# An FFT filter feeding a two-matmul block: where the second half of a complex product is formed

## The chip, the cores and the metric

The kernel runs on one core of one Trainium2 chip. The metric is device time in microseconds (us) of one execution; the median of three runs of the kernel before is 816.59 us (816.1 to 817.59). Engines are named as the profile names them: PE is TensorE (matmuls), PEld its weight loads, DVE is VectorE, ACT is ScalarE, POOL is GpSimd, SP is SyncE. POOL and SP do nothing here but issue DMAs. Each has its own DMA queue.

## The reference, cut to what matters

```python
def _attn_ref(x, filt_r, filt_i):              # x: (8, 3008, 256)
    X = np.fft.rfft(x, axis=1)                 # 1505 frequencies
    Y = X * (filt_r + 1j * filt_i)[None]       # complex product
    return np.fft.irfft(Y, n=3008, axis=1)

def _moe_ref(x, w_in, w_out, alpha):           # x: (24064, 256)
    h = x @ w_in                               # 256 -> 2048
    g = np.maximum(h, 0.0) + alpha * np.minimum(h, 0.0)
    return g @ w_out                           # 2048 -> 256
```

The output of the first, reshaped to 24064 rows, is the input of the second.

## The kernel before, in words

**The FFT of one batch** (`class Fft`; b counts 0 to 7) splits 3008 into 47 x 64 and 1505 frequencies into 24 groups ("k1"). It runs in pieces:

- `piece_a` (16 of them, L156): one matmul of the loaded input `xs` into one of the two PSUM buffers named psF, evicted by ACT into `asb`. After every fourth, `save_a` (L165) stores a quarter of `asb` to DRAM (`a_dram`) through SP's queue, 384 KB.
- `turn_a` (L169): four DMAs of 384 KB on SP's queue read `a_dram` back transposed into `at`, in runs of 512 bytes.
- `piece_b` (12, each two k1, L178): two matmuls give the spectrum in a psF buffer, real parts on partitions 0 to 63 and imaginary parts on 64 to 127. DVE multiplies it twice: `uu` by `filt_s`, `ww` by `filts_s`, 128 x 512 each. For these batches `filt_s` holds the filter's real part on both halves and `filts_s` the imaginary part on both.
- `piece_c` (12, L189): per k1, two accumulating matmuls, `twi_s` with `uu` and `twx_s` with `ww`. `twx_s` is `twi_s` with its halves exchanged and one sign turned, so the second matmul completes the complex product inside the inverse transform. ACT evicts the sum to `v`.
- `turn_c` (4, L202): after each third `piece_c`, four DMAs of 96 KB on SP's queue store that part of `v` to `v_dram`. After the fourth, SP waits until all of these have landed and then loads `zt` in four DMAs of 384 KB (L214).
- `piece_d` (16, L216): four small matmuls from `zt`, evicted by ACT to `yT`. The first four need only the first of the four `zt` loads.

**The two-matmul block** (`class Block`) handles 48 blocks of 512 columns of `yT` (four of 384). `up(j)`, 16 per block, is two matmuls of 512 columns into a buffer hps; after every second one ACT copies the pair to fp16 (`gtb`, a ring of 17 buffers) and DVE does two `TENSOR_SCALAR` (L415) and one add over 1024 elements (L416). `down(q)`, one block later, is four matmuls of 256 columns that read `gtb`; ACT evicts to `osb` (three buffers) twice per block and SP stores it (L388).

**What sets the order.** Everything is written in program order by hand, and each engine works through its own list strictly in that order. The main loop has 768 steps; a step is one `up` and one `down`, followed by whatever `plan` holds for that step. `plan_fft` (L439) enters a batch's pieces: for batches b = 3 to 7, with p = 96 (b - 1), `piece_a` at p - 54 to p - 24 (every second step), `turn_a` at p - 22, `piece_b` at p + 6, p + 11, ... p + 61, each `piece_c` four steps behind its `piece_b`, the last `turn_c` at p + 66, `piece_d` from p + 91. Batch 1 has its `piece_b` every 2.5 steps (44 to 71), batch 2 every 5 (110 to 165). POOL's queue carries the loads of `xs` (`load_x`, L123): two DMAs for each quarter of the next batch, entered one step after the `piece_a` that frees the buffer. So the pieces of batch b + 1 overlap with those of batch b, and SP's queue takes the stores, turns and loads of both in the order in which the steps enter them.

Batch 0 (`class First`) has its own pieces, run before the main loop; it uses `twx_s` too (built by `cross`, L334).

Of the kernel before, what the change touches and what calls it, by code (L numbers as in the profile page):

```python
# [10 lines left out]
FP16 = mybir.dt.float16  # L11
# [5 lines left out]
NK1 = 24  # L17
D = 256
# [4 lines left out]
OP = mybir.AluOpType  # L23
# [41 lines left out]
def kernel(  # L65
# [10 lines left out]
    nc = tc.nc  # L76
# [9 lines left out]
    konst = ctx.enter_context(tc.tile_pool(name="konst", bufs=1))  # L86
    p_x = ctx.enter_context(tc.tile_pool(name="p_x", bufs=4))
    p_fft = ctx.enter_context(tc.tile_pool(name="p_fft", bufs=1))
    p_uw = ctx.enter_context(tc.tile_pool(name="p_uw", bufs=2))
    p_m = ctx.enter_context(tc.tile_pool(name="p_m", bufs=2))  # L90
    p_osb = ctx.enter_context(tc.tile_pool(name="p_osb", bufs=3))
    psH = ctx.enter_context(tc.tile_pool(name="psH", bufs=2, space=bass.MemoryType.PSUM))
# [9 lines left out]
    wi3_s = konst.tile([96, 2 * N1], FP16, name="wi3_s")  # L102
    twf_s = konst.tile([128, NK1, 128], FP16, name="twf_s")
    twi_s = konst.tile([128, NK1, 128], FP16, name="twi_s")
    twx_s = konst.tile([128, NK1, 128], FP16, name="twx_s")
    filt_s = konst.tile([128, NK1, D], FP16, name="filt_s")
    filts_s = konst.tile([128, NK1, D], FP16, name="filts_s")
    al16 = konst.tile([16, 128], FP32, name="al16")
# [5 lines left out]
    wfx_s = konst.tile([2 * N1, 96], FP16, name="wfx_s")  # L114
    id16 = konst.tile([128, 128], FP16, name="id16")
    gtb = konst.tile([128, 17, 2, 512], FP16, name="gtb")
    yT = konst.tile([128, 2, 2 * NFFT], FP16, name="yT")

    def xrow(b, h, c):
# [3 lines left out]
    def load_x(b, c):  # L123
        xs = p_x.tile([2 * N1, 8 * D], FP16, name="xs")
        for h in range(2):
            nc.gpsimd.dma_start(out=xs[h * N1 : h * N1 + N1], in_=xrow(b, h, c))  # L126
        return xs
# [12 lines left out]
    def bank(wide=False):  # L140
        if wide:
            return psH.tile([128, 2, 512], FP32, name="hps")[:, 0]
        return psF.tile([128, 512], FP32, name="psF")


    class Fft:
# [31 lines left out]
        def piece_b(self, kp):  # L178
            px = bank().rearrange("p (k d) -> p k d", k=2)
            for kh in range(2):  # L180
                k1 = 2 * kp + kh
                nc.tensor.matmul(px[:, kh], twf_s[:, k1], self.at[:, k1], start=True, stop=True)  # L182
            uu = p_uw.tile([128, 2, D], FP16, name="uu")
            ww = p_uw.tile([128, 2, D], FP16, name="ww")
            nc.vector.tensor_mul(uu, px, filt_s[:, 2 * kp : 2 * kp + 2])  # L185
            nc.vector.tensor_mul(ww, px, filts_s[:, 2 * kp : 2 * kp + 2])  # L186
            self.uw[kp] = uu, ww

        def piece_c(self, kp, evict, pv=None):  # L189
            if kp == 0:  # L190
                self.v = p_fft.tile([128, NK1, D], FP16, name="v")
                self.zt = p_fft.tile([96, NH, D], FP16, name="zt")
            uu, ww = self.uw.pop(kp)
            if pv is None:
                pv = bank().rearrange("p (k d) -> p k d", k=2)
            for kh in range(2):
                k1 = 2 * kp + kh
                nc.tensor.matmul(pv[:, kh], twi_s[:, k1], uu[:, kh], start=True, stop=False)  # L198
                nc.tensor.matmul(pv[:, kh], twx_s[:, k1], ww[:, kh], start=False, stop=True)  # L199
            evict(self.v[:, 2 * kp : 2 * kp + 2], pv)  # L200

        def turn_c(self, q):  # L202
# [33 lines left out]
    class First(Fft):  # L236
# [27 lines left out]
        def piece_b(self, kp):  # L264
            hp = psH.tile([128, 2, 512], FP32, name="hps")
            px, pz = (hp[:, i].rearrange("p (k d) -> p k d", k=2) for i in range(2))
            for i, ps in enumerate((px, pz)):
                for kh in range(2):
                    k1 = 2 * kp + kh
                    for o in (0, 64):  # L270
                        nc.tensor.matmul(ps[o : o + 64, kh], twf_s[:, k1, 64 * i : 64 * i + 64],
                                         self.at[:, k1], start=True, stop=True)
            uu = p_uw.tile([128, 2, D], FP16, name="uu")
            ww = p_uw.tile([128, 2, D], FP16, name="ww")
            nc.vector.tensor_mul(uu, px, filt_s[:, 2 * kp : 2 * kp + 2])
            nc.vector.tensor_mul(ww, pz, filt_s[:, 2 * kp : 2 * kp + 2])
            self.uw[kp] = uu, ww
# [33 lines left out]
    for g in range(4):  # L311
        ka, kb = 6 * g, 6 * g + 6
# [9 lines left out]
    for q in range(2):  # L322
        nc.gpsimd.dma_start(
            out=wout_s[:, 8 * q : 8 * q + 8],
            in_=moe_w_out[1024 * q : 1024 * q + 1024].rearrange("(j p) d -> p j d", p=128))
# [3 lines left out]
    def warm(n):  # L329
        pw = psO.tile([128, 2, D], FP32, name="op")  # L330
        for _ in range(n):
            nc.tensor.matmul(pw[:, 0, 0:128], id16, id16, start=True, stop=True)

    def cross(ka, kb):  # L334
        nc.vector.tensor_copy(twx_s[0:64, ka:kb], twi_s[64:128, ka:kb])
        nc.vector.tensor_scalar(twx_s[64:128, ka:kb], twi_s[0:64, ka:kb], -1.0, None, OP.mult)
# [16 lines left out]
    for kp in range(12):  # L353
# [4 lines left out]
            f0.piece_b(kp + 2)  # L358
        if kp in (0, 3):
            cross(6 + 2 * kp, 12 + 4 * kp)  # L360
    for o in (0, 64):
        nc.gpsimd.dma_start(out=filts_s[o : o + 64], in_=filt_s[64:128])
    nc.gpsimd.dma_start(out=filt_s[64:128], in_=filt_s[0:64])
    warm(8)
    for i in range(4):
        f0.piece_t(i, both[i % 2], i % 2 == 1)
# [69 lines left out]
    def put(step, fn, *args):  # L436
        plan.setdefault(step, []).append((fn, args))

    def plan_fft(b, a0, ga, ta, b0, gap, d0, quarters=1):  # L439
        f = Fft(b)  # L440
        for i in range(16):
            put(a0 + ga * i, f.piece_a, i, on_act)
        for c in range(4):
            put(a0 + ga * (4 * c + 3), f.save_a, c)
            if b + 1 < NB:
                put(a0 + ga * (4 * c + 3) + 1,
                    lambda b=b, c=c: xc.update({(b + 1, c): load_x(b + 1, c)}))
        for q in range(quarters):
            w = NK1 // quarters
            put(ta, f.turn_a, nc.sync, w * q, w * q + w)  # L450
        for kp in range(12):
            put(int(b0 + gap * kp), f.piece_b, kp)
            put(int(b0 + gap * kp) + 4, f.piece_c, kp, on_act)
        for q in range(4):
            put(int(b0 + gap * (3 * q + 2)) + 5, f.turn_c, q)
        for i in range(16):
            put(d0 + min(i, 4) + 2 * max(i - 4, 0), f.piece_d, i, on_act)

    for g, t0, d0, gap, evs in ((1, 0, 4, 1, both), (2, 17, 24, 2, (on_dve,)), (3, 32, 40, 2, (on_act,))):
        for i in range(4):  # L460
            put(t0 + gap * i, f0.piece_t, 4 * g + i, evs[i % len(evs)])
            put(d0 + gap * i, f0.piece_d, 4 * g + i, evs[i % len(evs)])
    plan_fft(1, 16, 1, 32, 44, 2.5, 92, 4)
    plan_fft(2, 66, 2, 97, 110, 5, 187, 4)
    for b in range(3, NB):
        p = 96 * (b - 1)
        plan_fft(b, p - 54, 2, p - 22, p + 6, 5, p + 91)

    prev = None
    step = 0  # L470
# [43 lines left out]
```

## Time and profile before

| | |
|---|---|
| median of the runs | 816.59 us |
| the profiled execution: its own time, its span | 817.19 us, 815.4 us |
| granted TensorE clock, mean | 0.997 |
| busy: PE, DVE, ACT, POOL | 795.7, 620.2, 594.9, 49.7 us |
| inverse matmuls, L198 and L199 | 168 and 168 of 128 x 256, mean 273 and 272 ns |
| products, L185 and L186 | 84 and 84 of 128 x 512, mean 684 and 681 ns |
| HBM read and written | 55.67 and 46.66 MB |

The page gives one execution. "Busy" is the time in which an engine had at least one instruction under way; matmuls overlap in a pipeline, so the mean duration of one is longer than the distance between two starts. A timeline row gives start, duration, engine, line, what is written from what, how many instructions are merged in it, and in brackets the idle time ahead of it with what ended it. Rows of SPq and POOL are DMA issues, not transfers. A row of the windows view gives for a stretch of the span the busy time of each engine, then the granted clock, the busy share of the 16 DMA engines (above 1 when packets overlap) and GB/s.

### The profile page before, as it was taken

The page shows a single profiled execution, that of the slowest core. Times are in us where ns is not written, and L with a number is a line of the kernel's source. Part 1 is how long each engine was busy: PE and PEld are TensorE (multiplying, and loading weights), DVE is VectorE, ACT ScalarE, POOL GpSimd, SP SyncE. Part 2 cuts the span into 40 slices and gives each one's busy share as a digit, 9 for nine tenths or more (in the row PEclk, how much of TensorE's full clock was granted, in tenths as well). Part 3 has the DMA queues.
Part 4 walks back from the last instruction along what each step waited for, and adds up shares of the span by engine and source line. Part 5 has one row for each costly group of instructions (what it writes and reads, how often), then busy time and mean ns, then how long its engine had stood idle before and what let it go on. Part 6 is the DMA issues. An engine that isn't in the chain of part 4 may idle for free.

```text
span 815.4 us, 16040 instructions
## 1 busy us (share of the span) xinstructions
PE 795.7 (98%) x6117; PEld 557.1 (68%) x6117; DVE 620.2 (76%) x1377; ACT 594.9 (73%) x836; POOL 49.7 (6%) x99
## 2 busy tenths in 40 slices
PE   7889999999999999999999999999999999999997
PEld 6656667676667666776667766767666777776665
DVE  4876886788777887788777887788877788777773
ACT  3677778868777677777877777786777766686663
POOL 7401001000100001000100001000000000000000
PEclk9999999999999999999999999999999999999999
DMA  9977429623692247721584136832255121511111
GB/s 186 195 157 174 123 66 220 168 58 84 139 215 61 69 99 176 174 52 46 134 214 105 46 66 159 199 81 66 74 162 140 47 59 46 136 41 33 40 40 52
DMA packets 88757, 89.76 MB, mean 110 GB/s; under 512 B 8600, under 2 KB 79272, under 8 KB 88488
## 3 DMA queue, kind: packets, MB, share of 16 engines
q1 hardware_dynamic: 79512, 68.80, 31.2%
q0 software_dynamic: 9168, 19.93, 14.6%
q8 instruction: 48, 0.79, 0.4%
q14 instruction: 29, 0.24, 0.1%
HBM read 55.67 MB, written 46.66 MB: 125 GB/s over the span
## 4 chain that ended last, share of the span: by engine, by line
PE 86%; DVE 5%; ACT 3%; DMA 3%; issue 2%; SPq 1%; POOL 0%; ACTq 0%; DVEq 0%; POOLq 0%
PE op L425 37%; PE hps L406 37%; PE psF L162 3%; PE psF L221 2%; PE psF L182 2%; PE psF L199 2%; PE psF L198 2%; DVE gtb L416 1%; DVE m L415 1%; ACT gtb L412 1%; DMA v_dram<-v 1%; DMA xs<-in_x_dram 1%; DMA twf_s<-c_twf 1%; SPq L208 1%; ACT v L228 1%
## 5 line engine op out<-in xcount | busy, mean ns | idle before, releaser
L412 ACT ACTIVATE gtb<-hps 128x1024 f16<-128x1024 f32 (+1 forms) x384 | 384.8, 1003 | 118.1 <-PE hps L406 113.4
L425 PE MATMUL op<-wout_s,gtb 128*128 128x256 f16 x3008 | 451.1, 272 | 0.6 <-DVE gtb L416 0.6
L406 PE MATMUL hps<-yT,win_s 128*128 128x512 f16 (+1 forms) x1536 | 449.5, 374 | 1.9 <-ACT yT L228 1.5
L425 PEld LDWEIGHTS <-gtb 128*128 128x128 f16 x3008 | 293.1, 97 | 190.9 <-DVE m L415 1.4
L415 DVE TENSOR_SCALAR m<-gtb,alm_s 128x512 f16<-128x512 f16 (+1 forms) x768 | 233.8, 347 | 145.9 <-ACT gtb L412 144.2
L416 DVE TENSOR_TENSOR gtb<-gtb,m 128x1024 f16<-128x1024 f16 (+1 forms) x384 | 261.6, 681 | 23.4 <-PE hps L406 0.9
L406 PEld LDWEIGHTS <-win_s 128*128 128x128 f16 x1536 | 144.8, 98 | 32.9 <-issue 5.0
L228 ACT ACTIVATE asb<-psF 96x512 f16<-96x512 f32 x112 | 66.3, 592 | 35.6 <-PE psF L162 35.6
L228 ACT ACTIVATE v<-psF 128x512 f16<-128x512 f32 x84 | 50.2, 597 | 22.6 <-PE psF L199 22.6
L228 ACT ACTIVATE yT<-psF 128x376 f16<-128x376 f32 x120 | 58.1, 484 | 10.9 <-PE psF L221 10.7
L430 ACT ACTIVATE osb<-op 128x512 f32<-128x512 f32 x96 | 56.1, 585 | 6.1 <-issue 3.2
L126 POOL DMA_DIRECT2D xs<-in_x_dram x64 | 32.7, 519 | 443.1 <-PE psF L162 434.2
L185 DVE TENSOR_TENSOR uu<-psF,filt_s 128x512 f16<-128x512 f32 x84 | 57.4, 684 | 0.0
L186 DVE TENSOR_TENSOR ww<-psF,filts_s 128x512 f16<-128x512 f32 x84 | 57.2, 681 | 0.0
L162 PE MATMUL psF<-xs,wf_s 94*96 94x512 f16 x112 | 42.6, 381 | 2.6 <-ACT v L228 1.5
L221 PE MATMUL psF<-wi_s,zt 96*128 96x94 f16 x504 | 42.1, 204 | 1.9 <-DVE zt L231 1.2
L198 PE MATMUL psF<-uu,twi_s 128*128 128x256 f16 x168 | 41.2, 273 | 0.0
L199 PE MATMUL psF<-ww,twx_s 128*128 128x256 f16 x168 | 41.2, 272 | 0.0
L221 PEld LDWEIGHTS <-zt 96*128 96x128 f16 x512 | 35.4, 97 | 6.7 <-issue 2.0
L182 PE MATMUL psF<-at,twf_s 128*128 128x256 f16 x168 | 32.1, 273 | 0.5 <-DVE ww L186 0.2
L182 PEld LDWEIGHTS <-twf_s 128*128 128x128 f16 x168 | 15.4, 98 | 3.7 <-DVE ww L186 1.2
L199 PEld LDWEIGHTS <-twx_s 128*128 128x128 f16 x168 | 16.4, 98 | 1.8
(54 smaller groups left out, 193.1 us busy)
## 6 DMA issues: line engine op xcount, KB each, us to landing
out_dram<-osb SPq DMA_DIRECT2D x128, 128.0 KB
xs<-in_x_dram POOLq DMA_DIRECT2D x64, 188.0 KB, 4.9
a_dram<-asb SPq DMA_DIRECT2D x28, 384.0 KB
v_dram<-v SPq DMA_DIRECT2D x112, 96.0 KB
zt<-v_dram SPq DMA_DIRECT2D x28, 384.0 KB
at<-a_dram SPq DMA_DIRECT2D x20, 384.0 KB
at<-a_dram SPq DMA_DIRECT2D x32, 96.0 KB
filts_s<-filt_s POOLq DMA_DIRECT2D x2, 768.0 KB, 11.3
```

The lines of the kernel that those rows point to most:

```text
L162: nc.tensor.matmul(ps[0:96], wf1_s, xs[:, o : o + 512], start=True, stop=True)
L182: nc.tensor.matmul(px[:, kh], twf_s[:, k1], self.at[:, k1], start=True, stop=True)
L185: nc.vector.tensor_mul(uu, px, filt_s[:, 2 * kp : 2 * kp + 2])
L198: nc.tensor.matmul(pv[:, kh], twi_s[:, k1], uu[:, kh], start=True, stop=False)
L199: nc.tensor.matmul(pv[:, kh], twx_s[:, k1], ww[:, kh], start=False, stop=True)
L221: nc.tensor.matmul(ps[:, m], self.zt[:, 8 * g + 4 * mh + m, dh * 128 : dh * 128 + 128], wi3_s, start=True, stop=True)
L228: nc.scalar.activation(o, i, AF.Copy)
L406: nc.tensor.matmul(self.hps[:, j % 2, 0:tn], win_s[:, kt, j * 128 : (j + 1) * 128], yT[:, kt, self.t0 : self.t0 + tn], start=(kt == 0), st ...
L412: nc.scalar.activation(g[:, :, 0:tn], self.hps[:, :, 0:tn], AF.Copy)
L415: nc.vector.tensor_scalar(m[:, i, 0:tn], g[:, i, 0:tn], 0.0, a, OP.min, OP.mult)
L416: nc.vector.tensor_add(g[:, :, 0:tn], g[:, :, 0:tn], m[:, :, 0:tn])
L425: nc.tensor.matmul(self.op[:, si % 2], self.gts[k][:, 128 * si : 128 * si + 128], wout_s[:, k], start=(k == 0), stop=(k == 15))
```

## The change

For batches b = 1 to 7 the complex product is now finished before the inverse matmul. `filts_s` holds the imaginary part on the lower half and its negative on the upper. `piece_b` forms `ww` first and `uu` second; two DMAs on POOL's queue (64 KB each) then copy each half of `ww` onto the other half of a new tile `sw`. A new `piece_s` adds `sw` to `uu` on DVE. `piece_c` keeps one matmul per k1, with `twi_s`. `piece_s` and `piece_c` come later than before: five and nine steps behind `piece_b` in batch 1, eight and thirteen in the others, so the last `turn_c` of b = 3 to 7 moves from p + 66 to p + 75. `piece_d` and `turn_a` stay where they were. Batch 2 has its `piece_b` every 4.5 steps. The loads of `xs` for b + 1 come no earlier than p - 32, p - 29, p - 26, p - 23. `twx_s`, now only used by batch 0, lies in a part of `gtb` that the main loop first writes in its second block; the negation of the filter half is done on DVE at steps 17 to 26, and the copy of its real half moves to step 29.

```diff
-    p_uw = ctx.enter_context(tc.tile_pool(name="p_uw", bufs=2))
+    p_uw = ctx.enter_context(tc.tile_pool(name="p_uw", bufs=3))
...
-    twx_s = konst.tile([128, NK1, 128], FP16, name="twx_s")
...
+    twx_s = gtb[:, 14:17].rearrange("p a b c -> p (a b c)").rearrange("p (k m) -> p k m", m=128)
...
-            uu = p_uw.tile([128, 2, D], FP16, name="uu")
+            uu = p_uw.tile([128, 2, D], FP16, name="uu", bufs=4)
             ww = p_uw.tile([128, 2, D], FP16, name="ww")
+            sw = p_uw.tile([128, 2, D], FP16, name="sw")
+            nc.vector.tensor_mul(ww, px, filts_s[:, 2 * kp : 2 * kp + 2])
             nc.vector.tensor_mul(uu, px, filt_s[:, 2 * kp : 2 * kp + 2])
-            nc.vector.tensor_mul(ww, px, filts_s[:, 2 * kp : 2 * kp + 2])
-            self.uw[kp] = uu, ww
+            for o in (0, 64):
+                nc.gpsimd.dma_start(out=sw[o : o + 64], in_=ww[64 - o : 128 - o])
+            self.uw[kp] = uu, sw
+
+        def piece_s(self, kp):
+            uu, sw = self.uw[kp]
+            nc.vector.tensor_add(uu, uu, sw)
...
-                nc.tensor.matmul(pv[:, kh], twi_s[:, k1], uu[:, kh], start=True, stop=False)
-                nc.tensor.matmul(pv[:, kh], twx_s[:, k1], ww[:, kh], start=False, stop=True)
+                nc.tensor.matmul(pv[:, kh], twi_s[:, k1], uu[:, kh], start=True, stop=True)
...
-    for o in (0, 64):
-        nc.gpsimd.dma_start(out=filts_s[o : o + 64], in_=filt_s[64:128])
-    nc.gpsimd.dma_start(out=filt_s[64:128], in_=filt_s[0:64])
+    nc.gpsimd.dma_start(out=filts_s[0:64], in_=filt_s[64:128])
...
-    def plan_fft(b, a0, ga, ta, b0, gap, d0, quarters=1):
+    def plan_fft(b, a0, ga, ta, b0, gap, lag, d0, quarters=1, x0=0):
...
-                put(a0 + ga * (4 * c + 3) + 1,
+                put(max(a0 + ga * (4 * c + 3) + 1, x0 + 3 * c),
                     lambda b=b, c=c: xc.update({(b + 1, c): load_x(b + 1, c)}))
...
             put(int(b0 + gap * kp), f.piece_b, kp)
-            put(int(b0 + gap * kp) + 4, f.piece_c, kp, on_act)
+            put(int(b0 + gap * kp) + lag - max(4, lag - 8), f.piece_s, kp)
+            put(int(b0 + gap * kp) + lag, f.piece_c, kp, on_act)
         for q in range(4):
-            put(int(b0 + gap * (3 * q + 2)) + 5, f.turn_c, q)
+            put(int(b0 + gap * (3 * q + 2)) + lag + 1, f.turn_c, q)
...
-    plan_fft(1, 16, 1, 32, 44, 2.5, 92, 4)
-    plan_fft(2, 66, 2, 97, 110, 5, 187, 4)
+    def neg(ka, kb):
+        nc.vector.tensor_scalar(filts_s[64:128, ka:kb], filt_s[64:128, ka:kb], -1.0, None, OP.mult)
+
+    for i in range(4):
+        put(17 + 3 * i, neg, 6 * i, 6 * i + 6)
+    put(29, lambda: nc.gpsimd.dma_start(out=filt_s[64:128], in_=filt_s[0:64]))
+    plan_fft(1, 16, 1, 32, 44, 2.5, 9, 92, 4)
+    plan_fft(2, 66, 2, 97, 110, 4.5, 13, 187, 4)
     for b in range(3, NB):
         p = 96 * (b - 1)
-        plan_fft(b, p - 54, 2, p - 22, p + 6, 5, p + 91)
+        plan_fft(b, p - 54, 2, p - 22, p + 6, 5, 13, p + 91, 1, p - 32)
```

More of the change, by code (lines that the diff above doesn't have):

```diff
@@ L192, in piece_c @@
                 self.zt = p_fft.tile([96, NH, D], FP16, name="zt")
-            uu, ww = self.uw.pop(kp)
+            uu, _ = self.uw.pop(kp)
             if pv is None:
@@ L272, in piece_b @@
                                          self.at[:, k1], start=True, stop=True)
-            uu = p_uw.tile([128, 2, D], FP16, name="uu")
+            uu = p_uw.tile([128, 2, D], FP16, name="uu", bufs=4)
             ww = p_uw.tile([128, 2, D], FP16, name="ww")
```

## The prediction, on record before the result

> **What bounds the kernel now.** I read the page's busy times and slices first, then the timeline of PE, of DVE and of SP's queue.
>
> ```profile
> PE 795.7 (98%) x6117; PEld 557.1 (68%) x6117; DVE 620.2 (76%) x1377; ACT 594.9 (73%) x836; POOL 49.7 (6%) x99
> ...
> PE   7889999999999999999999999999999999999997
> ...
> DVE  4876886788777887788777887788877788777773
> ```
>
> PE is busy from the second tenth of the kernel to the end, and the chain that ended last is 86% PE. Fewer matmuls mean less time as long as nothing else comes late. How much less is read from the starts in PE's timeline, since the 272 ns of one matmul are a pipeline's latency:
>
> ```profile
> 299.90 0.27 PE L198 MATMUL psF<-uu,twi_s 128*128 128x256 f16 x1
> ...
> 300.01 0.27 PE L199 MATMUL psF<-ww,twx_s 128*128 128x256 f16 x1
> ...
> 300.12 0.27 PE L198 MATMUL psF<-uu,twi_s 128*128 128x256 f16 x1
> ...
> 300.23 0.27 PE L199 MATMUL psF<-ww,twx_s 128*128 128x256 f16 x1
> ```
>
> Four starts, 0.109 us apart: one inverse matmul costs PE 0.109 us.
>
> DVE's 76% is a mean over stages. In batch 1, whose `piece_b` comes every 2.5 steps, its timeline shows rows without a gap:
>
> ```profile
> 97.48 0.68 DVE L185 TENSOR_TENSOR uu<-psF,filt_s 128x512 f16<-128x512 f32 x1
> 98.08 0.68 DVE L186 TENSOR_TENSOR ww<-psF,filts_s 128x512 f16<-128x512 f32 x1
> 98.68 0.61 DVE L415 TENSOR_SCALAR m<-gtb,alm_s 128x512 f16<-128x512 f16 x2
> 99.32 0.69 DVE L416 TENSOR_TENSOR gtb<-gtb,m 128x1024 f16<-128x1024 f16 x1
> 99.93 0.68 DVE L185 TENSOR_TENSOR uu<-psF,filt_s 128x512 f16<-128x512 f32 x1
> ```
>
> Start to start: 0.60 per product, 0.64 for the two L415, 0.61 for L416, so 1.20 for one `piece_b` and 1.25 for two steps of the block. Between 87.2 and 116.6 DVE is busy 27.89 of 29.40 us.
>
> The third limit is hidden: SP's queue where batch 2 ends and batch 3 is turned.
>
> ```profile
> 220.53 2.19 SPq L388 DMA_DIRECT2D out_dram<-osb  x3
> 222.82 0.52 SPq L167 DMA_DIRECT2D a_dram<-asb  x1
> 223.44 3.50 SPq L208 DMA_DIRECT2D v_dram<-v  x4
> 229.65 1.72 SPq L214 DMA_DIRECT2D zt<-v_dram  x4
> 231.41 7.20 SPq L174 DMA_DIRECT2D at<-a_dram  x4
> ```
>
> The last `v` goes out, `zt` comes in, and only then is `at` turned. On PE the last `piece_a` starts at 220.05 and the first `piece_d`, which reads `zt`, at 237.21.
>
> **The change part by part.** Made against the profiled execution's own 817.19 us, which is 0.6 above the median of the runs.
>
> *The matmuls taken away.* 7 batches x 24 = 168 at 0.109 us: **-18.3**. Weight loads (98 ns) stay below the 109 ns, so they don't take their place. If another wait takes the room, nothing is saved; the three next items are such waits.
>
> *The turn of the order on SP's queue.* `turn_a` of batch b + 1 stands at p + 74 in b's count; the last `turn_c` moves from p + 66 to p + 75. So SP's order becomes: last store of `asb`, `turn_a`, `v`, `zt`; `piece_d` still starts at p + 91. This meets five batches, b = 2 to 6 (batch 2: 170, 173 and 187; batch 7 has no turn behind it, batch 1 has eleven steps between). Time t runs from the start of the last `piece_a` (step 72):
> - The store of `asb` issued at 222.82, t = 2.8, behind three output stores; two stores of such a row take 1.2 instead of 2.2, so 1.8 in the two batches with two.
> - `turn_a` waits until it has landed. A store at 147.21, also beside `xs` loads, let the turn start at 151.53, 4.3 later: t = 7.1. (Bounds: 3.5, as for the last `v` stores at 695.22, which let `zt` start at 698.69; 5.7 for 608.16 to 613.87, behind `zt`.)
> - First packets 0.9 after the issue (issue 330.60, traffic from 331.5). Then 4 x 384 KB = 1.57 MB:
>
> ```profile
> 331.50:338.50 7.00, 7.00 (x70) 5.47 (x69) 4.61 (x13) 5.41 (x10) 0.00 (x0) 1.00 1.14 227
> ```
>
>   The DMA engines are full; 1.57 MB at 227 GB/s are 6.9 us: t = 14.9.
> - `v`, 4 x 96 KB in the same queue behind it: 1.7 at that rate, about 0.4 until the wait ends: t = 17.0.
> - The first `zt` load: 0.9 to its packets, 0.39 MB at 227 GB/s 1.7, some 0.3 to land: t = 19.9, or 18.9 with two stores.
>
> Before, `piece_d` started 17.16, 15.44, 16.72, 15.44, 16.72 us after the last `piece_a`; the one `piece_c` now in between (two matmuls) adds 0.2. PE stands still for 2.5, 3.3, 3.0, 3.3, 3.0: **+15.1**. A stall adds in full, as PE's order is fixed. With the lower bound of the store (0.8 less) and no time to land (0.7 less) it is 15.1 - 5 x 1.5 = 7.6; with the upper bound and 1.5 more where `xs` loads, now packed into steps 64 to 73, share the engines, 15.1 + 5 x 2.9 = 29.6. I take 15, made of this kernel's rows under the same load.
>
> *The adds on DVE.* No row has this shape. L416 takes 681 ns for 1024 elements and its 768 form 560, so 512 extrapolates to some 440, or 0.36 start to start like its neighbours; bounds 0.30 (one L415) and 0.60 (a product). I take 0.36. Batch 1: per `piece_b` 1.25 x 1.25 + 1.20 + 0.36 = 3.1 us on DVE against 2.5 x 0.87 + 0.44 = 2.6 on PE (0.87 is a step without FFT pieces, 319.59 to 320.46). Eleven intervals, nine adds: DVE's work grows from 30.4 to 33.6, and may lag some 2 us at the end (in the rows shown by 1.3 more than at the start): 31.5 instead of 29.4. PE gains 2.6 there by the first item; instead it loses 2.1: **+4.7** (3 to 7).
>
> In batches 2 to 7 a period is 2.5 x 1.25 + 1.20 + 0.36 = 4.7 on DVE against 5 x 0.87 + 0.44 = 4.8 on PE in the stretch with neither `piece_a` nor `piece_d` (353 to 376: DVE 19.88 of 23.00). 98%: it holds, with little pushes: **+1** (0 to 5). `piece_c` waits for the add, four or five steps behind it: hidden.
>
> *The exchange through POOL.* Two issues of 0.505 us after `ww`, then landing. `filt_s` to itself, 768 KB, landed in 5.3; `xs` loads of 188 KB in 3.5 to 5.4 where nothing queued, 6.7 to 7.9 at 130 to 137. The add would wait with DVE's whole list behind it. It stands eight steps on, about 7.6 us; in batch 1 five steps, some 5.5. From `ww`'s end 0.1 + 0.5 + 3.5 = 4.1: hidden, with 1.4 to spare in batch 1. I cost it at **0** (upper bound: 2 us for each of batch 1's twelve, 24, if they land like 130 to 137). The `xs` loads moved behind the last exchange have over 60 steps until use.
>
> [...]
>
> *The rest.* Four negations at steps 17 to 26 (rows of 64 x 768: 420 ns; DVE is busy 7.84 of 11.00 us at 61 to 72): 0. One 768 KB copy less at 40 us: 0. `twx_s` in `gtb` and more buffers: 0, no wait on either is on PE's list.
>
> Sum: 817.2 - 18.3 + 15.1 + 4.7 + 1.0 = **819.7**; on the scale of the median 0.6 less, **819**.
>
> **The rivals.**
> 1. *The cover of `zt` holds better (faster).* One mechanism, the chain from the last store of `asb` to the first `zt`. For it: each link is a separate row, and the sum of five slacks could be generous. Each us less gives back 5: 0.5 less makes the kernels equal (2.5 / 5), 0.8 less makes the new one faster by over 0.2%. At the lower bound, 817.2 - 18.3 + 7.6 + 3 = 809; with `zt` in time throughout 804. Against it: `turn_a` alone fills 7 of 15 to 17 us, and nothing in these rows passes what is ahead of it in SP's queue (the store at 322.60, behind the `zt` loads of 319.20, let its turn start only at 330.60).
> 2. *The transfers are slower than their rows (slower).* `xs`, output stores and the turn meet in one stretch: 29.6 instead of 15.1 gives 834. For it: the share above 1 at 331.5 to 338.5.
> 3. *The exchanges land late.* 840 or more, DVE waiting at its adds. For it only 130 to 137; against it the low DMA share, 0.22, where most of them run (353 to 376).
> 4. *The cut doesn't shorten PE at all*, being bound by weight loads: excluded by 98 against 109 ns.
>
> A stall of 3 us could also cost clock. Here the granted clock is 0.96 in the first 40 us and 0.99 to 1.00 in later windows, where the longest wait on PE's list is 1.1 us, so no row shows it. [...] I leave it out of the sum.
>
> **How the numbers follow.** Forecast (815 to 826): 0.42, of which 0.15 lies within 0.2% of before (about what a measurement of this kernel can tell from no change). Rival 1 (below 815): 0.34. Rival 2 (826 to 836): 0.16. Rival 3: 0.08. Faster 0.34, same 0.15, slower 0.42 - 0.15 + 0.16 + 0.08 = 0.51. The likeliest case's own range is 815 to 826; the range for 8 in 10 runs from rival 1's 804 to 831, leaving out rival 3 and the upper half of rival 2.
>
> **What would show it.** PE's idle time at L221 should be put down to the `zt` load, five times, 2 to 4 us each; SP's list should show L174 ahead of the last `turn_c` and its `zt`. Batch 1's `piece_b` starts should lie 3.1 us apart, with PE waiting for DVE's products. The add should be 0.44 us long, without idle time ahead of it that a DMA ended. It would be wrong if `zt` never ends a PE wait, or if the adds wait for `sw`.

## The result and the profile after

The changed kernel takes **852.33 us** (median of four runs, 849.95 to 854.19) beside 816.73 us for the kernel before in the same comparison: a ratio of 1.0434, 95% interval 1.04 to 1.0467. It is slower, as the prediction held slightly more likely than not, but by 36 us and not by 2, and outside the predicted range. The profiled execution took 854.19 us, its span is 852.4 us and its mean granted clock 0.976 (before: 0.997).

The same parts of the page of the changed kernel, with the row of the small inverse matmuls added:

```profile
PE 789.6 (93%) x5949; PEld 544.3 (64%) x5949; DVE 650.7 (76%) x1465; ACT 596.9 (70%) x836; POOL 137.1 (16%) x266
...
PE   6889987999969999699996999969999999999997
...
DVE  4787995599747997489873898739987699867773
...
PEclk8999999999989999899998999979999999999999
...
L227 PE MATMUL psF<-wi_s,zt 96*128 96x94 f16 x504 | 44.3, 212 | 38.5 <-DMA zt<-v_dram 36.6
```

The 168 matmuls are gone (6117 to 5949), but PE now has notches: behind the start-up four slices of 6 among the nines, five slices of 21 us apart, that is one per batch. DVE shows a 4 or 3 in the same four slices, so the two wait together, and the granted clock drops to 8 or 7 there as well. The last row names the wait: of the 38.5 us that PE stood idle ahead of `piece_d`, 36.6 were ended by the load of `zt`. In the timeline of PE these are six places, one for each of batches 1 to 6 (left out are 7.46 at 459.76 and 7.36 at 563.03):

```profile
148.80 0.43 PE L227 MATMUL psF<-wi_s,zt 96*128 96x94 f16 x4 [4.83 <-DMA zt<-v_dram]
...
252.56 0.49 PE L227 MATMUL psF<-wi_s,zt 96*128 96x94 f16 x4 [6.67 <-DMA zt<-v_dram]
...
357.22 0.49 PE L227 MATMUL psF<-wi_s,zt 96*128 96x94 f16 x4 [7.58 <-DMA zt<-v_dram]
...
662.00 0.34 PE L227 MATMUL psF<-wi_s,zt 96*128 96x94 f16 x4 [2.73 <-DMA zt<-v_dram]
```

Batch 6's wait is the size that was predicted for all (2.5 to 3.3); batches 2 to 5 pay more than double, and batch 1, which was to pay nothing, pays 4.83. The same stretch of SP's queue as in the prediction, where batch 2 ends and batch 3 is turned, now reads:

```profile
231.35 0.52 SPq L167 DMA_DIRECT2D a_dram<-asb  x1
237.52 2.39 SPq L174 DMA_DIRECT2D at<-a_dram  x4
240.01 3.35 SPq L214 DMA_DIRECT2D v_dram<-v  x4
248.68 1.72 SPq L220 DMA_DIRECT2D zt<-v_dram  x4
```

The order is the one forecast: the turn (L174) ahead of `v` and `zt`. What is new is the first gap, 231.35 to 237.52: the turn waits 6.2 us for the store to land, where 4.3 was assumed. POOL's list in the same stretch shows what shares the DMA engines with that store:

```profile
222.00 1.03 POOL L189 DMA_DIRECT2D sw<-ww  x2 [3.04 <-DVE ww L186]
223.02 3.13 POOL L126 DMA_DIRECT2D xs<-in_x_dram  x6
229.46 1.00 POOL L126 DMA_DIRECT2D xs<-in_x_dram  x2 [3.31 <-PE psF L162]
```

Six loads of `xs` (188 KB each) go out in one bunch directly behind the last exchange, and two more just before the store. In the windows view, whose last three columns are granted clock, DMA share and GB/s, the DMA engines are then full (1.00) up to the store's issue:

```profile
223.00:231.30 8.30, 8.30 (x59) 5.53 (x58) 5.72 (x15) 7.34 (x11) 4.16 (x9) 1.00 1.00 207
```

Where a batch's time went is read from the start of its first `piece_d` to that of the next batch's, in us; the last row is the last experiment below, put here for comparison:

| | first `piece_d` of b = 1 | 1 to 2 | 2 to 3 | 3 to 4 | 4 to 5 | 5 to 6 | 6 to 7 | span |
|---|---|---|---|---|---|---|---|---|
| before | 140.2 | 97.0 | 96.7 | 95.8 | 96.7 | 95.8 | 92.9 | 815.4 |
| changed | 148.8 | 103.8 | 104.7 | 102.5 | 103.3 | 99.0 | 90.0 | 852.4 |
| last experiment | 142.7 | 95.3 | 94.2 | 93.3 | 94.2 | 93.3 | 90.0 | 803.5 |

The last column of batches is the only one in the changed kernel without a new wait, and it is 2.8 us shorter than before. So the cut itself works, and everything else takes it back.

### The profile page after: what moved, and what is told of

Read it like the earlier page. It is cut to its first block, busy times and chain, and to the rows that moved or that the text cites. A ratio compares the mean times of both kernels' runs of the same rounds, so it can differ in the third digit from the quotient of the medians.

```text
span 852.4 us, 16109 instructions
## 1 busy us (share of the span) xinstructions
PE 789.6 (93%) x5949; PEld 544.3 (64%) x5949; DVE 650.7 (76%) x1465; ACT 596.9 (70%) x836; POOL 137.1 (16%) x266
## 4 chain that ended last, share of the span: by engine, by line
PE 81%; DMA 7%; DVE 6%; ACT 2%; issue 2%; SPq 1%; POOL 0%; DVEq 0%; ACTq 0%; POOLq 0%
PE op L429 35%; PE hps L410 34%; PE psF L162 3%; DMA v_dram<-v 3%; DMA zt<-v_dram 3%; PE psF L227 3%; PE psF L205 2%; PE psF L182 2%; DVE m L419 2%; ACT gtb L416 1%; DVE gtb L420 1%; SPq L214 1%; DMA xs<-in_x_dram 1%; DVE ww L186 1%; DMA sw<-ww 1%
## 5 line engine op out<-in xcount | busy, mean ns | idle before, releaser
L410 PE MATMUL hps<-yT,win_s 128*128 128x512 f16 (+1 forms) x1536 | 454.3, 378 | 2.1 <-ACT yT L234 1.6
L419 DVE TENSOR_SCALAR m<-gtb,alm_s 128x512 f16<-128x512 f16 (+1 forms) x768 | 236.9, 350 | 148.9 <-ACT gtb L416 147.3
L189 POOL DMA_DIRECT2D sw<-ww x168 | 87.4, 525 | 501.2 <-DVE ww L186 492.2
L227 PE MATMUL psF<-wi_s,zt 96*128 96x94 f16 x504 | 44.3, 212 | 38.5 <-DMA zt<-v_dram 36.6
L194 DVE TENSOR_TENSOR uu<-uu,sw 128x512 f16<-128x512 f16 x84 | 35.1, 418 | 3.0 <-DMA sw<-ww 3.0
L205 PE MATMUL psF<-uu,twi_s 128*128 128x256 f16 x168 | 32.1, 273 | 1.9 <-DVE uu L187 1.3
L205 PEld LDWEIGHTS <-twi_s 128*128 128x128 f16 x168 | 16.1, 98 | 4.4 <-issue 2.0
```

What stands on the lines that cost most here:

```text
L189: nc.gpsimd.dma_start(out=sw[o : o + 64], in_=ww[64 - o : 128 - o])
L227: nc.tensor.matmul(ps[:, m], self.zt[:, 8 * g + 4 * mh + m, dh * 128 : dh * 128 + 128], wi3_s, start=True, stop=True)
L410: nc.tensor.matmul(self.hps[:, j % 2, 0:tn], win_s[:, kt, j * 128 : (j + 1) * 128], yT[:, kt, self.t0 : self.t0 + tn], start=(kt == 0), st ...
L419: nc.vector.tensor_scalar(m[:, i, 0:tn], g[:, i, 0:tn], 0.0, a, OP.min, OP.mult)
```

## The experiments

Theory **A**: the loss is made by the order on SP's queue, `turn_a` standing ahead of `v` and `zt`. Its rivals put the loss on what the change adds (exchanges, adds), or on the lag, which is the number of steps from a `piece_b` to its `piece_c`; each is described in the expectation that tests it. Later a second theory, **P** and **X** in the expectations, came up: that the bunched `xs` loads lengthen A's chain. All ratios are to the kernel before.

### The turn behind `zt`

```diff
-        plan_fft(b, p - 54, 2, p - 22, p + 6, 5, 13, p + 91, 1, p - 32)
+        plan_fft(b, p - 54, 2, p - 18, p + 6, 5, 13, p + 91, 1, p - 32)
```

> One number changed: for batches 3 to 7 the turn of `at` is entered at p - 18 instead of p - 22, so that on SP's queue it stands behind the last store of `v` and the loads of `zt` of the batch before. Theory A (the order on SP's queue: `v` and `zt` stand behind 1.57 MB of `at`): the waits of PE for `zt` in batches 2 to 6 go (4.8 us in batch 1 stay), and with them the stretches of low clock behind them: 805 to 815 us. Theory B (the DMA engines are overloaded by the exchanges and the bunched loads of `xs`, whatever the order): the waits stay at half or more, 830 us or above. Theory C (DVE is what bounds): no change, 850.

Measured: 813.87 us (812.45 to 815.86), ratio 0.9965 (0.9952 to 0.9977); faster than before. The waits view of PE, with sum, count and longest in us, has one wait for `zt` left, batch 1's:

```profile
PE psF L227 <- DMA zt<-v_dram: 4.4, 1, 4.4
```

One number in the plan takes 38 us away. A holds; what stays is batch 1, and two waits at a `piece_b`, the reader of `at` (1.67 us at 348, 2.51 at 538), since the turn now comes late.

### The schedule without the new product

Product and inverse matmuls as before the change (two accumulating matmuls, no exchange, no add), batch 1 with its old lag of four; steps of batches 2 to 7 as changed. Nothing of the result is left out.

```diff
-            for o in (0, 64):
-                nc.gpsimd.dma_start(out=sw[o : o + 64], in_=ww[64 - o : 128 - o])
-            self.uw[kp] = uu, sw
+            self.uw[kp] = uu, ww
...
-            nc.vector.tensor_add(uu, uu, sw)
+            pass
...
-                nc.tensor.matmul(pv[:, kh], twi_s[:, k1], uu[:, kh], start=True, stop=True)
+                nc.tensor.matmul(pv[:, kh], twi_s[:, k1], uu[:, kh], start=True, stop=False)
+                nc.tensor.matmul(pv[:, kh], twx_s[:, k1], ww[:, kh], start=False, stop=True)
...
-    plan_fft(1, 16, 1, 32, 44, 2.5, 9, 92, 4)
+    plan_fft(1, 16, 1, 32, 44, 2.5, 4, 92, 4)
```

> The product as before the change (two products, two inverse matmuls, no exchange, no add), but the new places in the plan: in batches 2 to 7 `piece_c` 13 steps behind `piece_b`, batch 2 at 4.5, the `xs` loads at p - 32 and on; batch 1 has its 4 steps as before. Theory A (order): the five waits for `zt` appear here too, 4 to 6.5 us each with 2 to 3 us of low clock each: 840 to 862 us. Theory B (the exchanges' traffic) and C (the adds on DVE): nothing of this is here, 815 to 823 us.

Measured in one execution: 854.6 us. Its waits view:

```profile
PE psF L224 <- DMA zt<-v_dram: 26.1, 5, 6.6
```

Five waits for `zt` (4.51, 6.60, 4.33, 6.53, 4.08), in batches 2 to 6, with all 168 matmuls still there and nothing new on DVE or POOL. So the plan's steps alone make the kernel this slow; the exchanges and adds are not needed for it. Batch 1, with its short lag, has no wait.

### A lag of nine

```diff
-    plan_fft(2, 66, 2, 97, 110, 4.5, 13, 187, 4)
+    plan_fft(2, 66, 2, 97, 110, 4.5, 9, 187, 4)
...
-        plan_fft(b, p - 54, 2, p - 22, p + 6, 5, 13, p + 91, 1, p - 32)
+        plan_fft(b, p - 54, 2, p - 22, p + 6, 5, 9, p + 91, 1, p - 32)
```

> Only the distance from `piece_b` to `piece_c` is changed in batches 2 to 7, from 13 steps to 9 (the add from 8 to 5), so the last `turn_c` comes at p + 71, ahead of the turn at p + 74. Theory A (order): as above, 805 to 816 us. Theory B (overload): 830 or above. Theory C (DVE): 850, or more, as the adds now follow their exchanges within five steps; if the exchanges land too late for five steps, DVE waits for `sw` show it.

Measured: 824.05 us (821.66 to 826.63), ratio 1.0092 (1.0069 to 1.0116), 8 us above what A expected. `v` is again ahead of the turn, and only batch 1's wait for `zt` is left (3.26 us). But the add now stands five steps behind its product, and DVE's waits show the new price:

```profile
DVE uu L194 <- DMA sw<-ww: 10.4, 14, 1.8
```

Shortening the lag gives the queue its order back and takes the exchange's cover away. Three waits of PE at a `piece_b` (7.1 us in all, 4.2 with the turn behind `zt`) come on top; the runs don't split the 8 us between the two.

### Filling PE while it waits

62 matmuls whose result nothing reads, ahead of the first `piece_d` of batches 2 to 5.

```diff
+    def fill(n):
+        pw = bank()
+        for _ in range(n):
+            nc.tensor.matmul(pw[:, 0:256], id16, filt_s[:, 0], start=True, stop=True)
...
+        if 2 <= b <= 5:
+            put(d0, fill, 62)
```

> Ahead of the first `piece_d` of batches 2 to 5, PE gets 62 matmuls of 256 columns into a spare use of a psF buffer, whose result nobody reads: 62 x 0.109 = 6.8 us of work in the place of the 6.7 to 7.6 us in which it waited for `zt`. Nothing else changes. If the idle time also costs clock (rows after it show 0.50 to 0.62 granted), the low clock goes and the kernel gains about 3 us per batch: 838 to 843 us. If the idle time costs only itself: 850 to 854.

Measured in one execution: 849.69 us, clock 0.990, 4.5 us less than the profiled execution of the changed kernel; the four runs of that one lie between 849.95 and 854.19, so the time alone shows no gain. The stretches do. In batch 3 the first to the fifth `piece_d` take 3.74 us instead of 5.32, as where nothing disturbs them: the clock loss is real and can be had back. The time is well above the 838 to 843 us expected, though. Waits of 0.74 to 1.91 us remain in batches 3 to 5, so the fill does not lie exactly in the gap; behind the 1.91 of batch 5 the clock fell all the same (0.57 over 4 us). A part of the shortfall stays unexplained.

### A lag of eleven

```diff
-    plan_fft(1, 16, 1, 32, 44, 2.5, 9, 92, 4)
-    plan_fft(2, 66, 2, 97, 110, 4.5, 13, 187, 4)
+    plan_fft(1, 16, 1, 32, 44, 2.5, 7, 92, 4)
+    plan_fft(2, 66, 2, 97, 110, 4.5, 11, 187, 4, 93)
...
-        plan_fft(b, p - 54, 2, p - 22, p + 6, 5, 13, p + 91, 1, p - 32)
+        plan_fft(b, p - 54, 2, p - 22 + (b == 3), p + 6, 5, 11, p + 91, 1, p - 32)
```

> The changed kernel with shorter lags: seven steps instead of nine in batch 1, eleven instead of thirteen in batches 2 to 7 (the add seven steps behind piece_b instead of eight), turn_a where it was (batch 3 one step later), so that it now stands behind the last zt, and batch 2's xs loads no earlier than steps 93 to 102. Theory A: no wait for zt in batches 2 to 6, none for at above 1 us; the add with seven steps waits little (five cost 10.4 us in 14 places, by nine steps of lag): 802 to 812 us. Rival (seven steps are still too few for the exchange beside xs loads): DVE waits 4 us or more for sw, 812 to 820 us.

Measured: 828.57 us (827.51 to 830.77), ratio 1.0151 (1.0137 to 1.0164): slower than both theories said. The waits for `zt` in batches 2 to 6 are gone and `sw` costs DVE 5.2 us in all, so both were wrong about what comes next. The timeline of PE around 391 us shows it:

```profile
388.91 0.38 PE L182 MATMUL psF<-at,twf_s 128*128 128x256 f16 x2
390.00 0.38 PE L205 MATMUL psF<-uu,twi_s 128*128 128x256 f16 x2
391.06 0.38 PE L162 MATMUL psF<-xs,wf_s 94*96 94x512 f16 x1 [0.68 <-ACT v L234]
```

With a period of five, a lag of eleven puts each `piece_c` one step behind a `piece_b`, and in places a `piece_a` right behind it: three users for two psF buffers. The third waits for an eviction. Twelve such waits add up to 8.2 us; in batch 3 to 4 PE is idle for 3.0 of 96 us against 0.9 of 94 in the second execution of the version with the turn behind `zt` (described next). Batch 1, with a lag of seven, costs more again: its first `piece_d` starts at 150.08, not at 145.51 as with the turn behind `zt`. A lag has to fit modulo the period, too.

### The turn directly behind `zt`, and a change that changed nothing

```diff
-    plan_fft(2, 66, 2, 97, 110, 4.5, 13, 187, 4)
+    plan_fft(2, 66, 2, 97, 110, 4.5, 13, 187, 4, 93)
...
-        plan_fft(b, p - 54, 2, p - 22, p + 6, 5, 13, p + 91, 1, p - 32)
+        plan_fft(b, p - 54, 2, p - 21 + 2 * (b == 3), p + 6, 5, 13, p + 91, 1, p - 32)
```

> The changed kernel, with turn_a one step later (for batch 3 three), directly behind the zt loads on SP's queue instead of ahead of the v stores; and the xs loads entered by batch 2's plan no earlier than steps 93, 96, 99, 102, so that they no longer run beside batch 1's v and zt. Theory A (the order on SP's queue makes the loss): PE waits for zt in none of batches 2 to 6; the turn has two or more steps more time before piece_b than with the turn at p - 18 (813.9 us, with 4 us of waits for at, which go), and batch 1's wait for zt (4.4 us with about 2 us of clock) goes: 803 to 811 us, ratio 0.984 to 0.993. Rival A' (the v stores and zt lie too late whatever the turn does, because of the lag of thirteen steps): waits of 1 to 3 us for zt in batches 2 to 6 remain, 812 to 820 us.

and the same `93` for batch 2 with the turn at p - 18:

> The changed kernel with turn_a at p - 18 (813.9 us before with that alone) and batch 2's xs loads no earlier than steps 93 to 102. Theory X (batch 1's zt is late because eight xs loads share the DMA engines with its v and zt): the wait for zt at batch 1's first piece_d falls from 4.4 to under 1 us and the clock stays at 1.00 there, 807 to 811 us. Rival (it is late because v itself is late, the stretch being bound by DVE): the wait stays at 3.5 us or more, 812 to 815 us.

Measured: 811.86 us (810.67 to 816.18), ratio 0.995 (0.9934 to 0.9967), and 811.25 us (810.19 to 815.46), ratio 0.9947 (0.9929 to 0.9965). Neither has a wait for `zt` in batches 2 to 6, so A holds against A', though the first version's time lies 0.9 above its range. Both keep batch 1's wait (4.86 and 3.48 us). That doesn't speak against X, because the second version's lists of instructions are the same, on every engine, as those of the first experiment: POOL's loads stand behind batch 1's last exchange in either case, and when one starts is set by the `piece_a` that frees its buffer, not by its step. So 813.87 and 811.25 are two measurements of one kernel, which is also the measure of how far such medians can be trusted. The first version's turn, up to three steps earlier, gains nothing that could be told from that.

### The `xs` loads at their old steps

```diff
-        plan_fft(b, p - 54, 2, p - 22, p + 6, 5, 13, p + 91, 1, p - 32)
+        plan_fft(b, p - 54, 2, p - 22, p + 6, 5, 13, p + 91)
```

> The changed kernel with the xs loads of batches 3 to 7 entered where the kernel before had them, one step behind each fourth piece_a, not packed into the last steps ahead of the turn. Theory P (the packed loads made the link from the store of asb to the turn longer): the time from the last piece_a to the turn falls from 6.2 to 7.6 us to 3.5 to 5 us in batches 2 to 5, the waits for zt there to 3 to 5 us, with less clock lost: 832 to 845 us. Rival (the link is long by itself, whatever loads run beside it): waits of 6 to 8 us remain, 850 to 855 us.

Measured: 847.65 us (844.51 to 849.51), ratio 1.037 (1.035 to 1.039). The loads now stand between exchanges. The link from the store of `asb` to the turn took 4.95, 4.64, 4.84, 7.77 and 3.33 us in batches 2 to 6 (changed kernel: 6.17, 7.47, 6.69, 7.65, 3.33), the waits 5.40, 5.62, 5.59, 7.54 and 2.83. P is right for three batches and the size was over-expected, since two loads still go out shortly before the store (226.44 before 228.34 in batch 2, 534.38 before 535.49 in batch 5, where the link didn't shorten at all; why batch 5 differs is not shown).

### Two cuts in batch 1

Without batch 1's adds, on the version with the turn at p - 18 (batch 1's output lacks `sw`):

```diff
-            nc.vector.tensor_add(uu, uu, sw)
+            if self.b > 1:
+                nc.vector.tensor_add(uu, uu, sw)
```

> The version with turn_a at p - 18 and batch 2's xs loads at steps 93 to 102 (811.3 us median, 809.9 in its profiled execution), with the adds of batch 1 left out: its part of the output then lacks sw; the exchange is still made. Theory D (DVE bounds batch 1's product stretch, each piece_b taking 2.83 us of its list): without the add's 0.34 a period falls to 2.5 us, the PE waits for DVE's products (1.36 us once, 0.85 and 0.49) go, and the stretch from the first piece_b to the last piece_c is 2 to 4 us shorter; batch 1's zt wait (3.5 us) does not grow. Time 805 to 808 us. Rival (PE, ACT or the DMAs bound that stretch): it is less than 1 us shorter, 809 to 811 us.

and, complete, with batch 2's `piece_a` and turn two steps later:

```diff
-    plan_fft(2, 66, 2, 97, 110, 4.5, 13, 187, 4, 93)
+    plan_fft(2, 68, 2, 99, 110, 4.5, 13, 187, 4, 93)
```

> The same version, complete, with batch 2's piece_a and its turn_a two steps later (68 to 98 and 99 in place of 66 to 96 and 97), so that its third store of asb is entered behind batch 1's last v and zt instead of ahead of them. Theory Q (batch 1's zt is late through what stands ahead of it on SP's queue and the full DMA engines): the wait falls from 3.5 us to 1 to 2.5 us, no clock is lost, 806 to 810 us. Rival (the v itself is late, or batch 2's turn now becomes late for its first piece_b at step 110): the wait stays, or as much comes back as a wait for at: 810 to 813 us.

Measured: 808.68 us in one execution, and 813.23 us (812.28 to 813.44), ratio 0.9953 (0.994 to 0.9967). Without adds, batch 1's first to last `piece_b` take 31.43 us, with them 34.25 (86.72 to 120.97): DVE's list bounds the stretch and the adds are worth 2.8 us there, D as expected. The time as a whole was 0.7 above its range, as a wait of 2.71 us for `zt` stayed and took clock with it (0.57 in the 4 us behind). Q falls: the store of batch 2 that stood directly ahead of batch 1's last `v` (134.43; it is the second one) now stands behind `zt` (141.44), and the wait was 4.43 us, not less.

### All `xs` loads behind the next batch's first exchange

```diff
-    plan_fft(2, 66, 2, 97, 110, 4.5, 13, 187, 4)
+    plan_fft(2, 66, 2, 97, 110, 4.5, 13, 187, 4, 111)
...
-        plan_fft(b, p - 54, 2, p - 22, p + 6, 5, 13, p + 91, 1, p - 32)
+        plan_fft(b, p - 54, 2, p - 22, p + 6, 5, 13, p + 91, 1, p + 7)
```

> The changed kernel with every xs load of batches 3 to 7 entered behind the next batch's first exchange (steps p + 7 to p + 16; for batch 2's plan 111 to 120), so that on POOL's list none can be issued while the stores, the turn and zt of the batch before are under way; turn_a stays ahead of v and zt. Theory P (the xs loads, which POOL issues in a bunch behind the last exchange whatever their step, made the store-to-turn link long): that link is 3 to 4 us in batches 2 to 6, as batch 6's 3.3 without xs loads, the waits for zt 2 to 3.5 us each, the sum 10 to 17 us, about the 15.1 predicted; 820 to 832 us. Rival (the link is long through the output stores or the stores of asb themselves): it stays at 5 us or more, 838 to 852 us.

Measured: 832.9 us (828.45 to 834.04), ratio 1.0188 (1.0155 to 1.0222), 19 us less than the changed kernel although the turn is still ahead of `zt`. SP's queue at the same place:

```profile
224.99 0.52 SPq L167 DMA_DIRECT2D a_dram<-asb  x1
228.24 2.09 SPq L174 DMA_DIRECT2D at<-a_dram  x4
...
239.33 1.72 SPq L220 DMA_DIRECT2D zt<-v_dram  x4
```

The store lets the turn go after 3.25 us instead of 6.17, and the DMA engines ahead of it are idle for most of the time:

```profile
217.00:225.00 8.00, 8.00 (x57) 5.37 (x55) 5.46 (x14) 6.97 (x11) 0.00 (x0) 1.00 0.38 101
```

The link is 3.25, 3.31, 3.35, 4.89 and 3.25 us in batches 2 to 6, and the waits for `zt` are 3.73, 4.06, 3.23, 4.80 and 2.73, in sum 18.6 beside the 15.1 predicted. Batch 1's falls to 1.15. P holds, though without any load batch 5 still has a link of 4.89, which nothing here explains; the median lies 0.9 above its range. The first to the fifth `piece_d` take 7.1 us more than undisturbed ones behind the waits of 3.73, 4.06 and 4.80, by a lower clock, which is more than the expectation had left for it.

### Both together

The same with the turn at p - 18 in place of p - 22.

> The same, with turn_a at p - 18, behind zt on SP's queue. The earlier attempt to keep the xs loads of batch 3 away from batch 1's v and zt (no earlier than steps 93 to 102) changed no engine's list, so that it ran the same kernel as the one with turn_a at p - 18 alone (813.9 and 811.3 us median). Here they do move. Theory X (batch 1's zt is late because of those loads): its wait falls from 3.5 to 4.4 us to 0.5 to 2.5 us, no clock is lost behind it, the turn waits for at go; 803 to 808 us. Rival (the loads don't matter there, or the exchanges that now stand behind xs loads make the adds wait): 809 to 815 us, with the wait for zt at 3.5 us or more, or DVE waiting over 3 us for sw.

Measured: **805.77 us** (805.29 to 806.03), ratio **0.987** (0.9855 to 0.9885), the fastest of all versions. Three lines of its page and one of its waits view:

```profile
PE 777.7 (97%) x5949; PEld 538.2 (67%) x5949; DVE 650.9 (81%) x1465; ACT 595.1 (74%) x836; POOL 137.8 (17%) x266
...
PE   6889989899999999999999999999999999999997
...
PEclk9999999999999999999999999999999999999999
```

```profile
PE psF L227 <- DMA zt<-v_dram: 1.1, 1, 1.1
```

No notch is left after the first fifth, the clock stays at 9 throughout, and of 36.6 us of waits 1.1 remain, in batch 1. X holds: the loads of `xs` were what made batch 1's `zt` late. No wait for `at` above 0.5 us is left either.

## Why the prediction was wrong, point by point

The mechanism was found, but the term of the sum that it makes, +15.1 for the chain from the last store of `asb` to the first `zt`, was mis-sized: it measured 31.8 in the five batches, 36.6 in six, and 10.2 of clock on top. Batch 2's, in us (the others differ by the output stores ahead and by POOL's loads):

| link | predicted | changed kernel | without `xs` loads beside it |
|---|---|---|---|
| last `piece_a` to the store's issue | 2.8 | 2.56 | 2.57 |
| store's issue to the turn's | 4.3 | 6.17 | 3.25 |
| turn's issue to `zt`'s | 9.9 | 11.16 | 11.09 |
| `zt`'s issue to `piece_d` | 2.9 | 3.88 | 3.92 |
| sum | 19.9 | 23.77 | 20.83 |
| PE's wait | 2.5 | 6.67 | 3.73 |

- **The step that failed**: "*A store at 147.21, also beside `xs` loads, let the turn start at 151.53, 4.3 later*". That row has one pair of loads beside it. The changed plan puts up to four pairs there, the prediction knew it ("now packed into steps 64 to 73") and still gave it 1.5 us in the upper bound alone, and 0 where it costed the move of the loads. It cost 2.9 us in this link of batch 2, and moving the loads away took the waits from 36.6 to 19.7 in sum, 3.7 of it in batch 1.
- A second miss in the same chain is its tail. "*some 0.3 to land*" for the first `zt` load and 0.4 for `v` are terms that no run shows by themselves, and the links they stand in were too short: `zt` took 3.7 to 4.3 us from issue to `piece_d` in all five batches instead of 2.9, with `xs` loads beside it or without, and the link ahead of it 9.9 to 11.3 instead of 9.9. Summed over the five batches of the changed kernel, the store's link is 9.8 us longer than predicted, the tail 7.8 (4.9 of it in the first `zt` load). The runs don't split this further. That the sum without `xs` loads beside the store, 18.6, comes near the predicted 15.1 is in part luck: the store's link is then shorter than the 4.3 assumed (3.4 less in sum) and the tail longer (some 7 more).
- "*batch 1 has eleven steps between*": failed. There is no turn there, but batch 2's stores and `xs` loads are, and the same chain without a turn took 14.3 us in the version with the turn moved (last `piece_c` at 130.71, `piece_d` at 145.03) where 10.8 were to be had. It cost 4.83 us in the changed kernel; the last experiment, with those `xs` loads moved, puts it down to them.
- "*I leave it out of the sum*": the clock. It has a row now. In the windows view of the changed kernel, the stretch around the end of batch 2's wait and behind it:

```profile
252.00:256.00 4.00, 3.44 (x18) 2.00 (x19) 0.00 (x0) 1.01 (x3) 0.00 (x0) 0.50 1.00 241
256.00:260.00 4.00, 4.00 (x30) 2.59 (x29) 1.31 (x3) 2.73 (x4) 0.00 (x0) 0.73 0.38 129
```

  PE works at 0.50 in the first window and at 0.73 in the second. From the first to the fifth `piece_d` batches 2 to 5 take 6.85, 5.32, 5.69 and 6.48 us instead of 4.15, 3.73, 4.15 and 3.73 where nothing disturbs them: 8.6 us. Batch 1 loses 1.6 more. That makes 10.2 for five stalls (batches 1 to 5). The prediction had no row for it; leaving it out of the range too was the wrong choice once stalls were in the sum.
- **Right**: 0.109 us per matmul. The fastest version saves 2.4 to 2.8 us in the five periods without a disturbance, and 2.6 was predicted (24 x 0.109). The add takes 418 ns (440 predicted) and 0.34 from start to start (0.36). Those five periods gain 12.7 us where 13.1 was predicted, so of the predicted +1 for DVE at most 0.4 was needed there.
- Batch 1's DVE: the 3.1 us per `piece_b` were right in the mean. The timeline of DVE shows a period with two steps of the block, 2.83 us from `ww` to `ww` (left out are `uu` and the block's three rows, which follow without a gap); one with four steps takes 4.08:

```profile
98.84 0.68 DVE L186 TENSOR_TENSOR ww<-psF,filts_s 128x512 f16<-128x512 f32 x1
...
101.33 0.42 DVE L194 TENSOR_TENSOR uu<-uu,sw 128x512 f16<-128x512 f16 x1
101.66 0.68 DVE L186 TENSOR_TENSOR ww<-psF,filts_s 128x512 f16<-128x512 f32 x1
```

  From first to last `piece_b`, eleven intervals, it takes 34.1 us, so 3.1 each, and before 32.8: 1.3 lost and 2.6 not gained, 3.9, where +4.7 (3 to 7) was predicted. The prediction's "29.4" spans only ten intervals (the twelfth `piece_b` of the kernel before starts at 120.08), and so its loss of 2.1 compares eleven with ten.
- The exchange: right at 0. The tile view of `sw`:

```profile
DMA to landing us min/median/max: 1.8/1.9/5.8
```

  In the median 1.9 us, where 3.5 was assumed, and only one add waited for it (3.05 us, in batch 1, for the last exchange there, issued at 126.18, with two `xs` loads directly behind it). In batch 1, with DVE's rows on end as above, these DMAs land in 2.0 us in the median (88 to 122 us), in the middle of batch 3's stretch (360 to 400) in 1.9.

The sum from the fastest version, whose profiled execution took 805.3: waits for `zt` 36.6 - 1.1 = 35.5, clock 10.2, and a start-up that reached batch 1's first `piece_b` at 88.65 in the changed kernel's execution and at 86.70 in the fastest version's, 2.0: together 853.0 of 854.2. The remaining 1.2 us are not placed.

## What to carry to other kernels

When an edit moves work to a later step, list for each queue what it now stands behind and what now stands beside it, and price the chain with the transfers that the edited plan puts there, not with those of the row it is taken from. A step number on POOL's list said little here: with batch 2's loads at step 93 every list was the same as without, and the loads moved past an exchange went out in one bunch behind it (six issues in 3.13 us, from 223.02). A predicted stall of the size of these may cost clock as well (1.5 to 2.8 us each in batches 1 to 5 of the changed kernel, none behind the 2.73 of batch 6), so its clock belongs into the range at least; and before giving up a change that loses, look for the number in the plan that turned an order round: here two edits of the plan turned +4.3% into -1.3%.

## What the runs showed of the hardware

- A stall's length alone does not tell whether the clock falls. In one execution, with all loads of `xs` moved, PE's waits of 3.73, 4.06 and 4.80 us were followed by 4 us at 0.57, 0.50 and 0.50, those of 3.23 and 2.73 by 1.00. Windows view of that version, behind the waits of 4.06 and 3.23 us:

```profile
343.38:347.38 4.00, 4.00 (x25) 2.83 (x26) 0.18 (x1) 1.78 (x3) 0.00 (x0) 0.50 1.02 289
```

```profile
443.02:447.02 4.00, 4.00 (x39) 2.88 (x40) 0.99 (x3) 2.82 (x6) 0.00 (x0) 1.00 0.89 287
```

  PE starts 25 matmuls in the first and 39 in the second. Nor is there a sharp lower end: waits of 1.91 us (the filled version, batch 5), 2.10 (the lag of eleven, batch 1) and 2.71 (without batch 1's adds) were followed by 0.57, 0.69 and 0.57, and one of 3.48 (second execution of the version with the turn moved) by 1.00. Behind the waits of 4.83 to 7.58 us in the changed kernel and of 3.73, 4.06 and 4.80 above, the next 4 us were at 0.50 to 0.60.
- The clock records in the traces show what does tell. In one execution the stretches at half clock start whole steps of 3.41 us apart (in the changed kernel at 148.90, 251.30, 353.70, 456.10 and 558.50, thirty steps from one to the next) and last one, two or three steps. In the changed kernel, from 100 us to the last 20, the clock fell behind the five steps at full clock in which PE was busy for 0.10, 0.00, 0.00, 0.00 and 0.58 us of the 3.41 (from 145.49, 247.89, 350.29, 452.69 and 555.09), and it held behind all others, the least busy of which had 1.41 (from 244.48), 1.78 (from 657.49) and 1.89 (from 142.08). The step need not be idle all through, nor is the limit sharp: the wait of 1.91 us in the filled version lies within one step by an estimate from the 0.57 behind it, which leaves at most 3.41 - 1.91 = 1.50 us of work there, and in the first 20 us the clock fell behind a step with 1.63 (changed, from 5.54) and one with 1.74 (before, from 14.79).
- For the version with all loads of `xs` moved, an estimate from the same step: its 0.57 over the 4 us from 243.25 is one step at half clock, so a step starts between 243.25 and 243.84 and one every 3.41 us from there. By that the wait of 4.06 us above left PE at most 0.5 us of work in the step ahead of the half clock, while the wait of 3.23 (from 439.79) fell into two steps with 1.4 us of work or more in each, and cost none. No run varied this by itself.
- A copy of 64 KB between two halves of SBUF on POOL's queue lands in 1.9 us in the median (5.8 at most; 6.5 in the fastest version, for one issued behind `xs` loads), while an `xs` load of 188 KB from HBM takes 6.3 in the median (4.9 before the change).
- A store of 384 KB lets the DMA that waits for it start after 3.25 to 3.35 us without `xs` loads beside it (4.89 in one batch of five), and after 6.2 to 7.7 with a bunch of them.
